# A weight conversion that begins one head pair later, with one of its steps in another cycle

## The chip, the cores and the metric

The kernel runs on one core of one Trainium2 chip. A core has five engines with a queue each: TensorE (PE), VectorE (DVE), ScalarE (ACT), GpSimd (POOL) and SyncE (SP, which here issues nearly all DMAs). The metric is the device time of one execution in microseconds; lower is better.

## The reference, cut to what matters

```python
# attention: batch 4, heads 8, sequence 576, head dimension 64
q_rot, k_rot = rotate(q), rotate(k)            # rotary embedding
scores = q_rot @ k_rot^T / 8
attn = softmax(scores)                         # row maximum subtracted first
x = (attn @ v) as (2304, 512)
# two FFN layers: weights 512 x 2048 and 2048 x 512, in float64
h = x @ w_in;   x = (h - tanh(h)) @ w_out
h = x @ w_in2;  out = (h * sigmoid(h)) @ w_out2
```

## The kernel before, in words

The 32 heads are taken as 16 **pairs** of heads. Each pair goes through five **cycles** (`z` from 0 to 4, here called cycle 1 to cycle 5). In a cycle TensorE multiplies the scores of two tiles (one in cycle 5; `sc`, L543), VectorE takes their row maxima (`row_max`, L548), ScalarE their exponentials (`exps`, L560). The score tiles have two buffers, so scores of one cycle wait for exponentials of the one before. In the same cycle TensorE transposes the probabilities of the cycles before (`tpp`, L453), which VectorE or ScalarE evict (L579, L581), multiplies them with v (L673), and `warm` (L519) issues transposes of the identity whose result nobody reads. GpSimd rotates q and k of a later pair (`rope_ops`, L416, L422, L426: three operations each). One rotation of pair 1 (numbered from 0) is done by VectorE instead. Its timeline in the first pair is one of the places that the change touches.

All engines take their work in the order in which this Python code issues it. Within a cycle the order is: scores and transposes, DMAs, early evictions, row maxima, VectorE's evictions, reciprocals, rotations, exponentials, late evictions, then `conv.run(n)`, then warm-up transposes and products with v.

`conv.run(n)` takes n steps of the **conversion** (class `Conv`, L92). The weights come as 64 float64 tiles of 128 by 512 (`keys`); of each, VectorE makes float32 bits in four operations: a single-operand one (`TENSOR_SCALAR`, L141) and three of two operands (L147, L152, L155). ScalarE squares the upper half (`magnitude`, L133). The first 16 tiles (`NEARLY`, j < 16) are then split into a high part by ScalarE (`high`, L166) and a low part by GpSimd (`low`, L170), and stay in SBUF. The later 48 go through DRAM (`wd`) and come back by `Fetch` (L200), which splits them (`split`, L254 and L255). The steps per cycle stand in `CONV_N`.

The FFN layers run in **ticks**: 160 of them, `tick(m)`. A tick multiplies one slice of h (`gemm_h`, L916, `hp`), issues its activations on ScalarE and VectorE, and then multiplies the slice of four ticks earlier with its second weight (`gemm_out`, L993, `acc`): for each of four column blocks three matmuls, high weight with high value, high weight with low value, low weight with high value. Before each use stands `need(key)`, which makes the fetcher go on until that weight has been issued. Otherwise the fetcher gets a number of turns per tick at the tick's end, and in the second part of the first layer only in some ticks:

```python
if TW[kb] == T and not (after and f % NH < 5):
    fetch.fill((2, int(f % NH > 3 or m < 5 * NH + NH), 3)[p])
```

For the ticks 40 to 47 that is one turn each, for 48 to 51 none, for 52 to 55 one each.

Of the kernel before, what the change touches and what calls it, by code (L numbers as in the profile page):

```python
# [29 lines left out]
def kernel(  # L30
# [34 lines left out]
    PE, ACT, DVE, POOL = nc.tensor, nc.scalar, nc.vector, nc.gpsimd  # L65
# [36 lines left out]
    class Conv:  # L102
# [33 lines left out]
        def bits(self, j):  # L136
            raw = self.raw[j]
            lo_w, hi_w = raw[:, :, 0], raw[:, :, 1]
            a = stage.tile([128, DM], I32, tag="wa", name="wa", bufs=3)
            af = self.val[j] = a.bitcast(F32)  # L140
            DVE.tensor_scalar(out=a, in0=hi_w, scalar1=3, scalar2=0x3FFFFFFF,  # L141
                              op0=ALU.logical_shift_left, op1=ALU.bitwise_and)
            yield
            if j < NEARLY:
                self.magnitude(j)
                yield
            DVE.scalar_tensor_tensor(out=a, in0=lo_w, scalar=29, in1=a,  # L147
                                     op0=ALU.logical_shift_right, op1=ALU.bitwise_or)
            if j >= NEARLY:
                self.magnitude(j)  # L150
            yield
            DVE.scalar_tensor_tensor(out=a, in0=hi_w, scalar=-0x40000000, in1=a,  # L152
                                     op0=ALU.bitwise_and, op1=ALU.bitwise_or)
            yield
            DVE.scalar_tensor_tensor(out=af, in0=self.mag.pop(j), scalar=TINY_HI * TINY_HI, in1=af,  # L155
                                     op0=ALU.is_ge, op1=ALU.mult)
            del self.raw[j]
            if j >= NEARLY:
                nc.sync.dma_start(out=wd[j], in_=self.val.pop(j))
                self.done = j + 1  # L160
            self.load(j + 3)
            yield
# [10 lines left out]
        def micro(self):  # L173

            late = []
            for j in range(self.n):
                if j >= NEARLY:
                    while late:
                        late.pop(0)()
                        yield  # L180
                while j >= self.allowed:
                    yield
                for n, _ in enumerate(self.bits(j)):
                    if late and n < 2:
                        late.pop(0)()
                    yield
                if j < NEARLY:
                    late += [lambda j=j: self.high(j), lambda j=j: self.low(j)]
# [137 lines left out]
    NP = B * NPAIR  # L326
# [3 lines left out]
    NPV = 4 * (NJ + 1)  # L330
    Q0 = 256
    WARM = (5, 5, 6, 2, 4, 1, 6)
    WARM_Z = (0, 6, 5, 5, 2, 0)
    ON_DVE = ((1, 0), (2, 0), (2, 1), (3, 0), (4, 0))
    QK_AT = (3, 2, 0)
    R_K = 3
    TURNED = mybir.DependencyInfo(mybir.DependencyClass.Sync, mybir.DependencyReason.DATA)
    E1_AT = 2
    PV_N = (4, 4, 6, 4, 2)
    CONV_N = (0, 0, 3, 2, 1), (2, 1, 1, 1, 1), (1, 1, 1, 1, 1)  # L340

    def attention(conv, on_rope_done, on_scores_near, on_scores_done):
        es_main, es_even, es_odd, es_rope, es_sc = (ExitStack() for _ in range(5))
# [38 lines left out]
        def load_v(i):  # L382
            b, c = divmod(i, NPAIR)
            vm = ap.tile([128, 2, NJ, D], F32, tag="vm", name="vm", bufs=2)

            vr = vr2[i % 2]
            nc.sync.dma_start(
                out=vm.rearrange("p h j d -> p h (j d)"),
                in_=v[b, 2 * c:2 * c + 2, 0:MAIN, :].rearrange("h (p j) d -> p h (j d)", j=NJ),
            )  # L390
            for h in range(2):
                nc.sync.dma_start(out=vr[half[h], h], in_=v[b, 2 * c + h, MAIN:S, :])
            v_t[i] = (vm, vr)
# [307 lines left out]
        pvq, rq, early, dve, late, stores = [], [], [], [], [], []  # L701

        def rope_push(i, ns=(4, 2, 3, 0, 1)):
            for n in ns:
                rq.extend((i, f) for f in rope_ops(i, n, POOL))
# [37 lines left out]
        conv.load(2)  # L743
        load_v(0)
        rope_push(1, (4, 3, 0, 1))
        i = z = 0
        while True:
            live, more = i < NP, i + 1 < NP
            qk_at = QK_AT[min(i, 2)]
            n0 = i * NTI + 2 * z  # L750
            gs = range(n0, n0 + (2 if z < NJ else 1)) if live else ()
            if more and z == 0:
                rope_upto(i + 1)
            early.clear(), dve.clear(), late.clear()
            pu = (i, z - 2) if z > 1 else (i - 1, z + NJ - 1)
            has = 0 <= pu[0] < NP
            if more and z == 0:
                qk_alloc(i + 1)
            qk = more and z == qk_at
            nop = nc.sync  # L760

            if len(gs) > 1:
                scores(gs[0], 0)
                if has:
                    turn(p_turn(*pu, 1))
                scores(gs[0], 1)
                blk = block(i, z)
                if blk:
                    t = turn(blk[1])
                scores(gs[1], 0)  # L770
                if qk and not blk:
                    kt = qk_turn(i + 1, 0)
                    tk = turn(kt[1])
                scores(gs[1], 1)
                if has:
                    turn(p_turn(*pu, 0))
                if blk:
                    turn_behind(t, blk[0], nop)
                if qk and blk:
                    kt = qk_turn(i + 1, 0)  # L780
                    tk = turn(kt[1])
                if qk:
                    turn_behind(tk, kt[0], nop)
            else:
                for g in gs:
                    scores(g, 0)
                    scores(g, 1)
                if live and more:
                    b = qk_turn(i + 1, 1)
                    up, dn = (p_turn(*pu, w) for w in (1, 0))  # L790
                    t = turn(b[1], dn[:NJ])
                    turn(up[:NJ], dn[NJ:])
                    n = nop.nop()
                    order(t, n)
                    order(n, turn(b[0][:1]))
                    turn(up[NJ:], b[0][1:])
                elif has:
                    turn(*[p_turn(*pu, w) for w in (1, 0)])
                blk = block(i, z)
                if blk:  # L800
                    turn_behind(turn(blk[1]), blk[0], nc.sync)
            store()
            if live:
                if i and z == 1:
                    load_v(i)
                if i == 0 and z == 1:
                    load_qk(2)
                if i + 3 < NP and z == 3:
                    load_qk(i + 3)
            if not n0:  # L810
                warm(WARM[5], idle)
                q_part(1, NJ)()
                warm(WARM[6], idle)

            for f in early:
                f()
            for g in gs:
                row_max(g)
            for f in dve:
                f()  # L820
            if i == 0 and z == 1:
                for f in rope_ops(1, 2, DVE):
                    f()
            if live and z == 2:
                recips(i, 0)
            if i and z == 0:
                recips(i - 1, 1)
            if more and z == (0 if i else 1) and i + 2 < NP:
                rope_push(i + 2)
            if live:  # L830
                for _ in range(4):
                    if rq:
                        rq.pop(0)[1]()
            if i == NP - 1 and z >= NJ - 1:
                on_scores_near(z)
            for g in gs:
                exps(g)
            for f in late:
                f()
            if live and z == NJ:  # L840
                pvq.extend((i, m) for m in range(NPV))
            conv.run(CONV_N[min(i, 2)][z] if i < NP else 0)
            if i * (NJ + 1) + z < len(WARM_Z):
                warm(WARM_Z[i * (NJ + 1) + z], idle)
            for _ in range(PV_N[z] if i < NP or z < 2 else NPV // 2):
                if pvq:
                    pv(*pvq.pop(0))
            if i >= NP - 1:
                store()
            if i == NP - 1 and z == 0:  # L850
                es_rope.close()
                es_even.close()
                on_rope_done()
            if i == NP - 1 and z == NJ:
                es_odd.close()
                es_sc.close()
                on_scores_done()
                on_tail()
            if not live:
                on_tail()  # L860
                if z > 1:
                    break
            i, z = (i, z + 1) if z < NJ else (i + 1, 0)
# [238 lines left out]
    conv = Conv()  # L1102
# [250 lines left out]
```

## Time and profile before

| | |
|---|---|
| median of 3 runs | 1067.76 us (1067.6 to 1068.08) |
| the profiled execution | 1068.44 us |
| its span, first to last instruction | 1066.7 us |
| PE busy | 1056.4 us, 99% of the span |
| DVE, ACT, POOL busy | 841.3, 631.7, 256.7 us |
| attention and its tail | to about 288 us |
| FFN layers | from then on, the first of their ticks in the tail |

Times in the rows below are microseconds from the span's start. A row of a timeline has the start, the duration, the engine, the line, the operation with the tiles that it writes and reads, their shape, and how many like instructions are merged in it; in brackets stands the idle time of the engine before it and what ended it. Line numbers are those of the kernel before; in the kernel after, lines 144 to 182 are one lower, and from 185 on two higher (746 to 820 three).

### The profile page before, as it was taken

To read this page: it belongs to the slowest core of one execution; us is meant where nothing else is said; L and a number is where in the kernel's file an instruction comes from. 1 tells how busy PE (TensorE), PEld (TensorE's weight loads), DVE (VectorE), ACT (ScalarE), POOL (GpSimd) and SP (SyncE) were. 2 spreads that over 40 slices of the span, in tenths; PEclk is the share of its full clock that TensorE was granted. 3 is DMA by queue.
4 is the path that set the end of the run, shared out by engine and by line. 5 is a ranking of instruction groups with operands and counts; after the bars stand their busy time and mean duration, and the time that the engine had idled before them with its cause. 6 is when DMAs were issued, how large, how long until landed. Compare 5 with 4: busy or idle time off the path is not lost.

```text
span 1066.7 us, 19432 instructions
## 1 busy us (share of the span) xinstructions
PE 1056.4 (99%) x7223; PEld 868.6 (81%) x7223; DVE 841.3 (79%) x1462; ACT 631.7 (59%) x1331; POOL 256.7 (24%) x324
## 2 busy tenths in 40 slices
PE   8999999999999999999999999999999999999998
PEld 6777777777688898888888898888888889999997
DVE  7889989988699778899999879977365357867775
ACT  5878777777667567768676666434343344334342
POOL 6888888882102001211020101400000000000000
PEclk9999999999999999999999999999999999999999
DMA  5334343333134323444555533756324212212142
GB/s 153 101 113 117 90 119 103 103 98 116 61 99 167 101 80 109 148 140 133 191 188 188 158 100 109 236 179 221 113 91 139 70 49 100 77 42 90 44 124 80
DMA packets 91278, 126.37 MB, mean 118 GB/s; under 512 B 16432, under 2 KB 57008, under 8 KB 91184
## 3 DMA queue, kind: packets, MB, share of 16 engines
q1 hardware_dynamic: 90592, 124.75, 36.7%
q8 instruction: 56, 0.92, 0.4%
q10 hardware_dynamic: 592, 0.39, 0.1%
q14 instruction: 38, 0.31, 0.1%
HBM read 88.93 MB, written 36.18 MB: 117 GB/s over the span
## 4 chain that ended last, share of the span: by engine, by line
PE 96%; ACT 2%; DVE 1%; issue 0%; SPq 0%; POOL 0%; DVEq 0%; POOLq 0%; ACTq 0%
PE hp L916 37%; PE acc L993 28%; PE M L1077 8%; PE sc L543 7%; PE x L673 6%; PE tpp L453 4%; PE tpq L453 2%; ACT p L560 1%; PE tpb L453 1%; PE acc L1221 1%; PE tpb L451 1%; DVE st L548 1%; PE x L519 0%; PE x L680 0%; PE x L677 0%
## 5 line engine op out<-in xcount | busy, mean ns | idle before, releaser
L916 PE MATMUL hp<-xh,w 128*128 128x512 f32 (+1 forms) x1280 | 388.0, 369 | 0.0
L916 PEld LDWEIGHTS hp<-xh,w 128*128 128x128 f32 x1280 | 234.5, 189 | 41.2 <-issue 0.8
L916 PE MATMUL hp<-xl,w 128*128 128x512 f32 (+1 forms) x640 | 236.0, 369 | 0.0
L927 ACT ACTIVATE t<-hp 128x512 f32<-128x512 f32 (+1 forms) x120 | 66.8, 557 | 243.3 <-PE hp L916 238.6
L993 PE MATMUL acc<-gh,w 128*128 128x512 f32 (+1 forms) x640 | 193.7, 368 | 0.0
L961 DVE TENSOR_TENSOR gl<-t,gh 128x512 fp32r<-128x512 f32 (+1 forms) x120 | 77.4, 645 | 111.8 <-ACT gh L959 111.5
L543 PE MATMUL sc<-kq 64*128 64x288 f32 (+1 forms) x640 | 151.4, 426 | 3.5 <-ACT p L560 2.6
L255 POOL TENSOR_TENSOR w<-wf,w 128x512 fp32r<-128x512 f32 x32 | 49.6, 1563 | 364.4 <-ACT w L254 364.4
L916 PEld LDWEIGHTS hp<-xl,w 128*128 128x128 f32 x640 | 120.8, 189 | 19.8 <-DVE xl L898 0.4
L993 PEld LDWEIGHTS acc<-gh,w 128*128 128x128 f32 x640 | 117.2, 189 | 20.3 <-issue 0.3
L548 DVE TENSOR_REDUCE st<-sc 128x1 f32<-128x576 f32 x144 | 107.5, 755 | 28.6 <-PE sc L543 23.4
L560 ACT ACTIVATE p<-sc,st 128x576 f32<-128x576 f32 x144 | 106.4, 740 | 37.7 <-DVE st L548 28.7
L993 PE MATMUL acc<-gl,w 128*128 128x512 f32 (+1 forms) x320 | 117.8, 368 | 0.0
L543 PEld LDWEIGHTS sc<-kq 64*128 64x128 f32 (+1 forms) x640 | 87.3, 176 | 36.1 <-ACT p L560 23.6
L453 PE MATMUL tpp<-ident,p 64*128 64x64 f32 x1248 | 101.7, 227 | 0.0
L453 PEld LDWEIGHTS tpp<-ident,p 64*128 64x128 f32 x1248 | 85.9, 139 | 4.1 <-DVE pt L581 2.5
L993 PE MATMUL acc<-w,gh 128*128 128x512 f32 x288 | 88.9, 390 | 0.0
L673 PE MATMUL x<-pt,vm 128*64 128x320 f32 (+1 forms) x512 | 79.5, 421 | 0.2 <-DVE xs L689 0.2
L959 ACT ACTIVATE gh<-t 128x512 fp32r<-128x512 f32 (+1 forms) x120 | 70.6, 588 | 6.2 <-PE acc L993 6.2
L1077 PE MATMUL M<-w,gh 128*128 128x256 f32 x384 | 70.3, 283 | 0.0
L993 PEld LDWEIGHTS acc<-gl,w 128*128 128x128 f32 x320 | 60.3, 189 | 9.9
L1077 PEld LDWEIGHTS M<-w,gh 128*128 128x128 f32 x384 | 61.8, 191 | 2.3
(140 smaller groups left out, 1950.7 us busy)
## 6 DMA issues: line engine op xcount, KB each, us to landing
raw<-in_moe_w_in_dram SPq DMA_DIRECT2D x32, 512.0 KB, 4.4
raw<-in_moe_w_out_dram SPq DMA_DIRECT2D x28, 512.0 KB, 3.7
xin<-xd SPq DMA_DIRECT2D x56, 256.0 KB, 4.1
wd<-wa SPq DMA_DIRECT2D x48, 256.0 KB, 2.2
wf<-wd SPq DMA_DIRECT2D x48, 256.0 KB, 4.0
pd<-xo SPq DMA_DIRECT2D x34, 256.0 KB, 2.7
xo<-pd SPq DMA_DIRECT2D x18, 256.0 KB, 5.2
xm<-in_q_dram SPq DMA_DIRECT2D x16, 256.0 KB, 3.0
```

The source lines that it names most:

```text
L255: (DVE if key[0] == 3 else POOL).tensor_tensor(out=w[:, 1].rearrange("p (a b) -> p a b", a=a), in0=src, in1=w[:, 0].bitcast(F32).rearrange ...
L453: t = PE.transpose(o, src, ident[r, r])
L543: PE.matmul(sc[o, e, 0:HALF], lhsT=kq[r, 1, c:c + n], rhs=kq[r, 0, k0:k0 + HALF], start=True, stop=True)
L548: DVE.tensor_reduce(out=st, in_=s_t[g][:, :, 0:HALF], op=ALU.max, axis=AX.XY, negate=True)
L560: ACT.activation(out=p.rearrange("p (e s) -> p e s", e=2), in_=sc[:, :, 0:HALF], func=ACTF.Exp, bias=st, accum_out=sum_t[i][:, n:n + 1])
L673: PE.matmul(x[o, 0:w], lhsT=vm[:, h, cc, :], rhs=ptm[:, cc, h, :], start=(cc == 0), stop=False)
L916: PE.matmul(hp, lhsT=w[:, a, ws], rhs=bb, start=(n == 0), stop=(n == 3 * KD - 1))
L927: ACT.activation(out=t, in_=hp, func=ACTF.Tanh, scale=0.5 if l else 1.0)
L959: ACT.activation(out=gh, in_=t, func=ACTF.Copy)
L961: DVE.tensor_tensor(out=gl, in0=t, in1=gh.bitcast(F32), op=ALU.subtract)
L993: PE.matmul(acc, lhsT=a, rhs=bb, start=(fi == 0 and n == 0), stop=(fi == NH - 1 and n == 2))
L1077: PE.matmul(prod_t[name][:, tt], lhsT=al[i], rhs=bw[j], start=(first and tt == 0 and x == 0), stop=(last and tt == nt - 1 and x == 2))
```

## The change

Four edits. In `bits`, ScalarE's squares of the first 16 tiles are issued in the same step as the single-operand operation, and not in a step of their own. In `micro`, the high part of the tile before gets a step of its own ahead of that. `CONV_N` becomes one step in cycle 5 of pair 0 and one step per cycle from then on; before, pair 0 had three, two and one steps in its cycles 3, 4 and 5, and pair 1 began with two. And VectorE's rotation of pair 1 is issued one operation per cycle in the cycles 1, 2 and 3 of pair 0, not as three in cycle 2, and the warm-up transposes of cycle 4 of pair 0 are 1 and not 5.

```diff
@@ bits @@
             DVE.tensor_scalar(out=a, in0=hi_w, scalar1=3, scalar2=0x3FFFFFFF,
                               op0=ALU.logical_shift_left, op1=ALU.bitwise_and)
-            yield
             if j < NEARLY:
                 self.magnitude(j)
-                yield
+            yield
@@ micro @@
-                for n, _ in enumerate(self.bits(j)):
-                    if late and n < 2:
+                if late:
+                    late.pop(0)()
+                    yield
+                for _ in self.bits(j):
+                    if late:
                         late.pop(0)()
                     yield
@@ tables @@
-    WARM_Z = (0, 6, 5, 5, 2, 0)
+    WARM_Z = (0, 6, 5, 1, 2, 0)
-    CONV_N = (0, 0, 3, 2, 1), (2, 1, 1, 1, 1), (1, 1, 1, 1, 1)
+    CONV_0 = (0, 0, 0, 0, 1)
@@ attention @@
         rope_push(1, (4, 3, 0, 1))
+        kr = rope_ops(1, 2, DVE)
         i = z = 0
...
-            if i == 0 and z == 1:
-                for f in rope_ops(1, 2, DVE):
-                    f()
+            if i == 0 and z < len(kr):
+                kr[z]()
...
-            conv.run(CONV_N[min(i, 2)][z] if i < NP else 0)
+            conv.run((1 if i else CONV_0[z]) if i < NP else 0)
```

On VectorE, pair 0, from the end of its preparation: `st` are the row maxima, `ak` and `bm` the rotation, `rr` the reciprocals, `wa` the conversion. Before:

```order
L508 TENSOR_TENSOR aq<-aq,p 128x2x3x64
L548 TENSOR_REDUCE st<-sc 128x1 x4
L416 TENSOR_TENSOR ak<-xm_192,csk 128x4x64
L422 TENSOR_TENSOR bm<-xm_192,csk 128x256
L426 TENSOR_TENSOR ak<-ak,bm 128x4x64
L548 TENSOR_REDUCE st<-sc 128x1 x2
L570 TENSOR_SCALAR rr<-sums 128x4
L571 RECIPROCAL rr<-rr 128x4
L141 TENSOR_SCALAR wa<-raw 128x512
L147 SCALAR_TENSOR_TENSOR wa<-raw,wa 128x512
L548 TENSOR_REDUCE st<-sc 128x1 x2
```

After:

```order
L510 TENSOR_TENSOR aq<-aq,p 128x2x3x64
L550 TENSOR_REDUCE st<-sc 128x1 x2
L418 TENSOR_TENSOR ak<-xm_192,csk 128x4x64
L550 TENSOR_REDUCE st<-sc 128x1 x2
L424 TENSOR_TENSOR bm<-xm_192,csk 128x256
L550 TENSOR_REDUCE st<-sc 128x1 x2
L428 TENSOR_TENSOR ak<-ak,bm 128x4x64
L572 TENSOR_SCALAR rr<-sums 128x4
L573 RECIPROCAL rr<-rr 128x4
L550 TENSOR_REDUCE st<-sc 128x1 x2
```

The three rotation operations stand each behind the maxima of one cycle, and no conversion step stands ahead of the maxima of cycle 4.

On VectorE from the maxima of cycle 4 of one pair to the first cycle of the next, as it then repeats from pair to pair. Before:

```order
L548 TENSOR_REDUCE st<-sc 128x1 x2
L581 COPY pr_690<-tpb 128x256
L581 COPY pt_689<-tpp 128x8x64
L141 TENSOR_SCALAR wa<-raw 128x512
L689 TENSOR_TENSOR xs<-x,rs 128x320
L548 TENSOR_REDUCE st<-sc 128x1
L581 COPY pt_836<-tpp 128x8x64 x2
L548 TENSOR_REDUCE st<-sc 128x1 x2
```

After:

```order
L550 TENSOR_REDUCE st<-sc 128x1 x2
L583 COPY pr_674<-tpb 128x256
L583 COPY pt_673<-tpp 128x8x64
L691 TENSOR_TENSOR xs<-x,rs 128x320
L550 TENSOR_REDUCE st<-sc 128x1
L583 COPY pt_818<-tpp 128x8x64 x2
L141 TENSOR_SCALAR wa<-raw 128x512
L550 TENSOR_REDUCE st<-sc 128x1 x2
```

The single-operand operation stood ahead of the one maximum of cycle 5 (and of the scaled output `xs`); it stands now behind the two evictions of that cycle and ahead of the maxima of the next pair's cycle 1.

On ScalarE in tick 51 of the FFN part: `t` is the tanh and `u` the square of the tick's `hp`, `xh` a split of the next input block, `w<-wf` the high part of a fetched weight. Names are shown with their numbers, which count up in the order of issue. Before:

```order
L897 ACTIVATE xh0_7699<-xin_7443 128x512
L927 ACTIVATE t_7703<-hp_7686 128x512
L931 ACTIVATE u_7705<-hp_7686 128x512
L959 ACTIVATE gh_7709<-t_7597 128x512
L940 ACTIVATE s_7713<-u_7705,sqa_70 128x512
L941 ACTIVATE mk_7714<-u_7705,ht2_71 128x512
L897 ACTIVATE xh1_7752<-xin_7444 128x512
L927 ACTIVATE t_7756<-hp_7739 128x512
```

After:

```order
L899 ACTIVATE xh0_7678<-xin_7421 128x512
L929 ACTIVATE t_7682<-hp_7665 128x512
L933 ACTIVATE u_7684<-hp_7665 128x512
L961 ACTIVATE gh_7688<-t_7575 128x512
L942 ACTIVATE s_7692<-u_7684,sqa_70 128x512
L943 ACTIVATE mk_7693<-u_7684,ht2_71 128x512
L256 ACTIVATE w_7698<-wf_7401 128x512
L899 ACTIVATE xh1_7745<-xin_7422 128x512
L929 ACTIVATE t_7749<-hp_7732 128x512
```

One row has come in, `w_7698`, behind the tick's own activations. On TensorE the matmuls that follow the tick's `hp` read that weight; before, they read one that was issued six ticks earlier (`w_7423`, in tick 45). Before:

```order
L916 MATMUL hp_7686<-xl3_7440,w_5709 128x512
L916 MATMUL hp_7686<-xh3_7439,w_5709 128x512
L993 MATMUL acc0_7352<-gh_7606,w_7423 128x512
L993 MATMUL acc0_7352<-gl_7607,w_7423 128x512
L993 MATMUL acc0_7352<-gh_7606,w_7423 128x512
```

After:

```order
L918 MATMUL hp_7665<-xl3_7418,w_5856 128x512
L918 MATMUL hp_7665<-xh3_7417,w_5856 128x512
L995 MATMUL acc0_7329<-gh_7583,w_7698 128x512
L995 MATMUL acc0_7329<-gl_7584,w_7698 128x512
L995 MATMUL acc0_7329<-gh_7583,w_7698 128x512
```

The matmuls stand where they stood; the weight that they read is issued just ahead of them. All other fetched weights are issued three ticks or more ahead of their use.

## Rows read from the trace of the kernel before

**Rows 1.** Timeline of PE in the first pair.

```profile
6.38 1.27 PE L519 MATMUL x<-ident 128*128 128x128 f32 x5
...
15.71 0.51 PE L543 MATMUL sc<-kq 64*128 64x288 f32 x1 [0.19 <-ACT p L560]
...
19.73 0.51 PE L543 MATMUL sc<-kq 64*128 64x288 f32 x1 [1.36 <-ACT p L560]
...
23.17 0.77 PE L519 MATMUL x<-ident 128*128 128x128 f32 x5
23.87 1.19 PE L543 MATMUL sc<-kq 64*64 64x288 f32 x8
```

**Rows 2.** Timeline of VectorE in the first pair.

```profile
14.03 1.48 DVE L548 TENSOR_REDUCE st<-sc 128x1 f32<-128x576 f32 x2 [1.72 <-PE sc L543]
15.43 0.97 DVE L416 TENSOR_TENSOR ak<-xm,csk 128x256 f32<-128x256 f32 x1
...
18.07 1.41 DVE L548 TENSOR_REDUCE st<-sc 128x1 f32<-128x576 f32 x2
```

**Rows 3.** Timeline of PE: first scores of cycles 1 and 2, pairs 2, 3, 14.

```profile
43.70 0.51 PE L543 MATMUL sc<-kq 64*128 64x288 f32 x1
...
47.12 0.51 PE L543 MATMUL sc<-kq 64*128 64x288 f32 x1
...
59.76 0.75 PE L543 MATMUL sc<-kq 64*128 64x288 f32 x2
...
63.38 0.51 PE L543 MATMUL sc<-kq 64*128 64x288 f32 x1
...
238.52 0.75 PE L543 MATMUL sc<-kq 64*128 64x288 f32 x2
...
242.16 0.51 PE L543 MATMUL sc<-kq 64*128 64x288 f32 x1
```

**Rows 4.** Timeline of VectorE around the starts of pairs 2 and 3.

```profile
43.26 1.29 DVE L581 COPY pt<-tpp 128x512 f32<-128x512 f32 x2
45.09 0.76 DVE L548 TENSOR_REDUCE st<-sc 128x1 f32<-128x576 f32 x1 [0.55 <-PE sc L543]
46.15 0.76 DVE L548 TENSOR_REDUCE st<-sc 128x1 f32<-128x576 f32 x1 [0.29 <-PE tpq L453]
...
57.58 0.97 DVE L141 TENSOR_SCALAR wa<-raw 128x512 int32<-128x512 int32 x1
...
59.53 1.27 DVE L581 COPY pt<-tpp 128x512 f32<-128x512 f32 x2
```

**Rows 5.** The line L141 over the span: ns shortest, median, longest.

```profile
L141 DVE TENSOR_SCALAR wa<-raw x64: 395/422/1522, 20.2 to 811.2; 128x512 int32<-128x512 int32 x64
```

**Rows 6.** Timeline of GpSimd around the start of pair 3.

```profile
57.53 0.73 POOL L426 TENSOR_TENSOR aq<-aq,bm 128x256 f32<-128x256 f32 x1
58.22 0.92 POOL L416 TENSOR_TENSOR aq<-xm,csq 128x256 f32<-128x256 f32 x1
...
60.59 1.28 POOL L170 TENSOR_TENSOR w<-wa,w 128x512 fp32r<-128x512 f32 x1
```

**Rows 7.** Timeline of ScalarE: first exponential of pair 2.

```profile
45.95 0.74 ACT L560 ACTIVATE p<-sc,st 128x576 f32<-128x576 f32 x1 [0.29 <-DVE st L548]
```

**Rows 8.** Timeline of ScalarE behind tick 51, and a weight's split in tick 52.

```profile
531.76 0.62 ACT L897 ACTIVATE xh<-xin 128x512 fp32r<-128x512 f32 x1
...
537.21 0.62 ACT L254 ACTIVATE w<-wf 128x512 fp32r<-128x512 f32 x1
```

**Rows 9.** Timeline of GpSimd, the low part of the same weight as in rows 8.

```profile
537.90 1.29 POOL L255 TENSOR_TENSOR w<-wf,w 128x512 fp32r<-128x512 f32 x1 [36.66 <-ACT w L254]
```

**Rows 10.** Timeline of PE in tick 51, from its first product with a second weight.

```profile
528.84 0.39 PE L993 MATMUL acc<-gh,w 128*128 128x512 f32 x1
...
529.29 0.62 PE L993 MATMUL acc<-gh,w 128*128 128x512 f32 x2
```

**Rows 11.** Stretches: busy us of PE, PEld, DVE, ACT, POOL; granted clock; DMA; GB/s.

```profile
1063.00:1066.70 3.70, 0.00 (x0) 0.00 (x0) 0.00 (x0) 0.00 (x0) 0.00 (x0) 0.88 0.46 126
```

## The prediction

> **What bounds the kernel now.** I read the page first: TensorE (PE) is busy for 99% of the span (the table above), so time is to be had only where PE stands still, and is lost wherever it is made to. The waits of PE and then its timeline show where that is. In the FFN layers its matmuls follow each other without a gap; in attention there are two places. The first is the first head pair: the scores of cycle 4 wait 1.36 us for an exponential [rows 1], and VectorE's timeline says why: the row maximum of cycle 3 starts at 18.07, behind three rotation operations that began at 15.43 [rows 2]. The second shows in no wait, only in a comparison of pairs: cycle 1 lasts 3.42 us in pair 2 (43.70 to 47.12), but 3.62 in pair 3 (59.76 to 63.38) and 3.64 in pair 14 (238.52 to 242.16) [rows 3]; all twelve pairs from 3 to 14 lie between 3.60 and 3.64. The reason is VectorE again: in pair 2's cycle 4 the single-operand step took 0.97 us where it mostly takes 0.42 [rows 4, 5], so that the two evictions of cycle 5 began 0.23 us ahead of the next pair's scores (59.53, 59.76) and not 0.44 (43.26, 43.70) [rows 3, 4]; PE's next transposes need the first eviction's bank. It took 0.97 because GpSimd was at work: GpSimd's operation ran from 57.53 to 58.26, and the step ended at 58.55, 0.29 after it [rows 4, 6].
>
> **The change part by part.**
> *Rotation, one step per cycle.* The first of the three operations goes into the 1.72 us that VectorE idles before 14.03 [rows 2]. The second stays ahead of cycle 3's maximum: 15.43 + 0.97 = 16.4, and the maximum can start when its scores are there, 1.39 us after the scores' start (43.70 to 45.09 [rows 3, 4]), so at 15.71 + 1.39 = 17.10, not 18.07. From such a start to the next scores it was 19.73 - 18.07 = 1.66 us [rows 1, 2], so cycle 4 starts at 18.76: 0.97 us won. The third operation lies behind that maximum, in time that the two conversion steps of cycles 3 and 4 leave empty.
> *Warm-up transposes 5 to 1 in cycle 4.* Five took 23.87 - 23.17 = 0.70 [rows 1]; four fewer are 0.56. They hid a wait before; with the maxima earlier there is none left to hide. Together 1.5; at least 0.6 if the maximum stays late, at most 1.9 with the small waits of cycle 4 gone too. I take **-1.6**.
> *The conversion begins one pair later.* Its operations are the same; only the first pair has fewer. In pairs 2 to 13 the one step that moves is the single-operand one: from ahead of cycle 5's maximum to behind cycle 5's evictions, ahead of the next pair's first maximum. Taking it away from its old place gives each of the twelve first cycles its 0.20 back (12 x 0.2 = 2.5 with the pairs as they are). What it meets at its new place decides. In pair 2's times: the evictions start at 59.76 - 0.44 = 59.32 and take 1.27, and an operation starts some 0.09 before the end of the one ahead, so the step comes at 60.50. GpSimd's operation at 58.22 is no longer held up and takes 0.73, not 0.92 [rows 6], so its subtraction for the weights starts at 60.59 - 0.19 = 60.40 and runs 1.28, to 61.68. It is ahead by 0.1; where the step came only 0.05 behind a GpSimd operation it waited it out [rows 4, 6], so it ends at 61.68 + 0.29 = 61.97. The row maximum behind it was wanted at 59.76 + 1.39 = 61.15 and starts at 61.88: 0.73 late. The chain to PE (0.86 to the exponential, its 0.74, some 0.14 more [rows 4, 7]) has 47.12 - 45.95 - 0.88 = 0.29 to spare, so PE is 0.44 late: the cycle takes 3.86, 0.24 more than now. The second maximum of that cycle waits for PE: it starts at 46.15, where 45.09 + 0.76 - 0.09 = 45.76 would do [rows 4], 0.39 to spare, so the reciprocals, from which GpSimd's round starts, slip by 0.73 - 0.39 = 0.34, 0.10 less than PE; in the next pair the subtraction ends 0.10 sooner, PE is 0.34 late, and there it stays: 3.76, or 0.14 more than now. 0.24 + 11 x 0.14 = **+1.8**. The bounds are -2.5 (the step gets through first) and +2.9 (0.24 each time).
> The Trainium skill, SBUF — State Buffer, section "Who interferes with whom", speaks against the new place: whichever of the two engines issues first holds the shared pair of ports for its whole instruction and the other fully blocks. The rows agree (an end 0.29 after GpSimd's); by it, too, the price hangs on the 0.1 alone. The sum by rule and by rows is one.
> *The backlog.* Attention now ends with weight 15 unfinished, and all 48 later weights are converted five steps later. Weight 15 itself is needed at tick 11 and emitted at tick 6. Most fetched weights are split one or two ticks later and still ticks ahead of use. One is not: the last second-half weight of the first FFN, ("out", 15). Its split was emitted in tick 45; now the fetcher has no turn left between ticks 48 and 51 (it gets none for the first four units of a block there), so it is emitted on demand in tick 51, directly before its first matmul: the order shows it behind tick 51's tanh and squares on ScalarE. Those wait for tick 51's own products, so the copy runs where ScalarE now does its next work, 531.76 [rows 8], to 532.38; GpSimd follows 0.69 after the copy's start and takes 1.29 (537.21, 537.90 [rows 8, 9]): 532.45 to 533.74. The third matmul of the group reads the low half; it started at 529.29, the first at 528.84 [rows 10]. With 0.1 for the signal (an estimate) the first can start at 532.48, 3.6 late, and the third at 533.84, 4.55 late. Forced conversion steps may hold GpSimd for a few tenths: up to 5.2. I take **+4.6**. Behind it on PE is everything else; nothing later gives it back, since PE has no idle time to shrink.
> *Sum.* -1.6 + 1.8 + 4.6 = +4.8. On the profiled execution's 1068.44 us (span 1066.7 and 1.7 around it) that is 1073.2; its time was 0.7 above the median, and on the median of 1067.76 it is **1072.5 us**.
>
> **Rivals.**
> *The step gets through before GpSimd (not slower).* My 0.1 us is made of several rows; if the subtraction starts 0.15 later than I have it, or the evictions end sooner, the step takes 0.42, ends at 60.9 before the maximum is wanted at 61.15, and each of twelve pairs wins 0.2 without loss: -1.6 - 2.5 + 4.6 = +0.5, so 1068.3. The timing repeats from pair to pair (3.60 to 3.64), so it is all of them or none. The 0.05 that decided in pair 2 speaks against it.
> *The clock falls in the pause of tick 51.* PE stands 3.6 us there. The trace has no fall between two matmuls, only one after the last: in 1063.0 to 1066.7 PE does nothing and the granted clock is 0.88 on the mean [rows 11]; with 1.0 and 0.5 as its two levels (2.4 and 1.2 GHz) it fell some 0.9 us before the end, 2.8 into that stretch. At the start five transposes still took 1.27 at 6.38, against 0.77 later [rows 1], so a low stretch could last 6.4 us and cost half of it: 1072.5 up to 1075.7.
> The Trainium skill, TensorE: Matmul & The Clock Gate, section "What's actually happening", has an idle array back at half its clock; no pause of this length lies between matmuls in this trace.
> *The weight is there in time.* If the split did not bind (ScalarE free earlier than its order allows), the sum is -1.6 + 1.8 = +0.2, 1068.0; with the step through as well, 1063.7. It needs the copy done by 528.84, before the products that stand ahead of it; the order leaves no way for that. That the first pair does not get shorter is no rival of its own: it adds 1.
>
> **How the numbers follow.** Forecast 0.54, with 1071.0 to 1073.8 as its own range (first pair 0.6 to 1.9, the pairs 1.2 to 2.9, the weight 4.4 to 5.2). Step through first: 0.24. Clock falls: 0.10. Weight in time: 0.08, half of it faster. Something else: 0.04. About 0.2%, 2.1 us, is what can be told from no change: slower means above 1069.9. Slower 0.54 + 0.10 + 0.02 = 0.66; same 0.24 + 0.04 + 0.01 = 0.29; faster 0.05. The range reaches from the step's rival to the lower part of the clock's: 1067.6 to 1074.4, which leaves out the faster cases and the longest low stretch.
>
> **What would show it.** Right: the waits of PE get two new rows of 3.6 and 0.9 us at L995, for the copy at L256 and the subtraction at L257; no wait of over 1 us stays in the first pair, whose second pair starts 1.6 us sooner; the step at L141 lasts 1.3 to 1.5 us in twelve pairs and overlaps the subtraction at L169; first cycles take 3.7 to 3.9. Wrong: steps of 0.4 us and first cycles of 3.42 (the first rival), no wait at L995, or a granted clock under 1.0 around 535.

## The result, and the profile of the kernel after

The kernel after takes 1074.74 us (median of 4 runs, 1074.6 to 1074.97) against 1067.92 of the kernel before (4 runs): the ratio is 1.0064, with a 95% interval of 1.0047 to 1.0082. It is slower, as forecast, but by 6.8 us and not by 4.7. The profiled execution of after took 1074.68 us with a span of 1072.9, 6.2 us longer than the span before; the rest of the difference is the 0.5 by which the profiled execution of before lay above its median.

The waits of PE in the kernel after show the two new rows at L995 and two more things.

```profile
PE sc L545 <- ACT p L562: 5.0, 16, 0.6
PE acc L995 <- ACT w L256: 3.4, 1, 3.4
PE x L521 <- POOL ident masks.py:199: 1.3, 1, 1.3
PE tpq L455 <- SPq L796: 0.9, 1, 0.9
PE acc L995 <- POOL w L257: 0.6, 1, 0.6
```

No wait of the first pair is over 1 us now (the 1.3 at L521 stands ahead of it, and stood there before). The first row had 5 waits of 2.6 us in all before; 11 of its 16 are new, each ahead of the scores of cycle 2, in the pairs 3 to 12 and 14. PE's timeline gives the places that answer to [rows 1, 3, 10]: first scores of pairs and cycles, the first product of the FFN layers, and tick 51.

```profile
8.86 1.25 PE L545 MATMUL sc<-kq 64*128 64x288 f32 x8
...
24.46 0.51 PE L545 MATMUL sc<-kq 64*128 64x288 f32 x1
...
57.00 0.51 PE L545 MATMUL sc<-kq 64*128 64x288 f32 x1
...
60.86 0.51 PE L545 MATMUL sc<-kq 64*128 64x288 f32 x1 [0.36 <-ACT p L562]
...
73.49 0.51 PE L545 MATMUL sc<-kq 64*128 64x288 f32 x1
...
77.26 0.51 PE L545 MATMUL sc<-kq 64*128 64x288 f32 x1 [0.29 <-ACT p L562]
...
221.28 0.27 PE L455 MATMUL tpq<-ident,aq 64*128 64x64 f32 x1 [0.95 <-SPq L796]
...
270.91 0.50 PE L918 MATMUL hp<-xh,w 128*128 128x512 f32 x1
...
528.61 0.39 PE L918 MATMUL hp<-xh,w 128*128 128x512 f32 x1
532.43 0.50 PE L995 MATMUL acc<-gh,w 128*128 128x512 f32 x1 [3.43 <-ACT w L256]
532.77 0.40 PE L995 MATMUL acc<-gl,w 128*128 128x512 f32 x1
533.78 0.93 PE L995 MATMUL acc<-gh,w 128*128 128x512 f32 x2 [0.62 <-POOL w L257]
534.51 0.63 PE L995 MATMUL acc<-gl,w 128*128 128x512 f32 x1
534.93 1.06 PE L995 MATMUL acc<-gh,w 128*128 128x512 f32 x2
535.79 0.63 PE L995 MATMUL acc<-gl,w 128*128 128x512 f32 x1
```

Pair 0 takes 24.46 - 8.86 = 15.60 us; before it took 17.65 (9.63 to 27.28). Pair 3's first cycle takes 3.86, where it took 3.62 [rows 3], and pair 4's 3.77. The FFN layers begin at 270.91; before they began at 270.94, so all of the attention part comes out even in these two executions. Two things that differ from one execution of a kernel to the next are in that: pair 0 begins 0.77 sooner (8.86 against 9.63; 9.45 in a second profile of the kernel after, below), and pair 12 loses 1.1 to a delayed DMA issue (last section). In tick 51 (which begins at 526.12, as before [rows 10]) the first product starts at 532.43 and the third at 533.78. From 534.51 on the starts lie 0.42 to 0.43 apart (534.51, 534.93; two of them to 535.79), where full speed is 0.23. The windows show why: granted clock in the column behind POOL.

```profile
526.12:531.56 5.44, 2.88 (x13) 2.06 (x11) 4.43 (x8) 3.91 (x8) 0.00 (x0) 1.00 0.90 291
531.56:534.00 2.44, 0.95 (x3) 0.51 (x4) 2.44 (x3) 1.33 (x3) 1.28 (x1) 1.00 0.08 31
534.00:537.50 3.50, 3.50 (x10) 2.72 (x10) 2.88 (x5) 0.00 (x0) 0.00 (x0) 0.52 0.40 106
537.50:543.00 5.50, 5.50 (x25) 4.54 (x24) 3.60 (x8) 2.28 (x5) 0.00 (x0) 0.99 1.00 357
```

PE's clock stood at 1.0 while PE waited and until 534, and then went to its lower level (0.5, 1.2 GHz) for some 3.4 us, in which PE was busy without a gap. Ticks 51 and 52 together take 17.12 us and not 10.88, 6.24 more: 4.49 from the late third product (533.78 against 529.29 [rows 10]) and 1.75 from the clock. That is as much as the spans differ by.

VectorE's timeline at the start of pair 3, which answers to [rows 4], and under it GpSimd's, which answers to [rows 6]:

```profile
56.56 1.29 DVE L583 COPY pt<-tpp 128x512 f32<-128x512 f32 x2 [0.22 <-PE tpp L455]
57.76 1.45 DVE L141 TENSOR_SCALAR wa<-raw 128x512 int32<-128x512 int32 x1
59.13 1.41 DVE L550 TENSOR_REDUCE st<-sc 128x1 f32<-128x576 f32 x2
```

```profile
56.97 0.72 POOL L428 TENSOR_TENSOR aq<-aq,bm 128x256 f32<-128x256 f32 x1
57.65 1.28 POOL L169 TENSOR_TENSOR w<-wa,w 128x512 fp32r<-128x512 f32 x1
```

The subtraction starts 0.11 ahead of the single-operand step and ends at 58.93; the step ends at 59.21, 0.28 after it, and the row maximum starts 2.13 after the pair's first scores (57.00).

### The profile page after: what moved, and what is told of

It reads as the page before. It is cut to its first block, busy times and chain, and to the rows that moved or that the text cites. A ratio compares the mean times of both kernels' runs of the same rounds, so it can differ in the third digit from the quotient of the medians.

```text
span 1072.9 us, 19417 instructions
## 1 busy us (share of the span) xinstructions
PE 1055.7 (98%) x7219; PEld 868.3 (81%) x7219; DVE 847.4 (79%) x1462; ACT 628.9 (59%) x1331; POOL 249.3 (23%) x324
## 4 chain that ended last, share of the span: by engine, by line
PE 89%; DVE 4%; issue 3%; ACT 2%; POOL 1%; DMA 0%; SPq 0%; ACTq 0%; POOLq 0%; DVEq 0%
PE hp L918 36%; PE acc L995 26%; PE M L1079 7%; PE sc L545 6%; PE x L675 5%; PE tpp L455 3%; ACT p L562 1%; DVE pt L583 1%; DVE wa L141 1%; PE tpq L455 1%; DVE st L550 1%; PE acc L1223 1%; PE tpb L455 1%; PE tpb L453 1%; DMA wf<-wd 0%
## 5 line engine op out<-in xcount | busy, mean ns | idle before, releaser
L995 PE MATMUL acc<-gh,w 128*128 128x512 f32 (+1 forms) x640 | 195.1, 370 | 4.0 <-ACT w L256 3.4
L995 PEld LDWEIGHTS acc<-gh,w 128*128 128x128 f32 x640 | 117.9, 190 | 25.4 <-ACT w L256 3.8
L257 POOL TENSOR_TENSOR w<-wf,w 128x512 fp32r<-128x512 f32 x32 | 45.8, 1440 | 355.6 <-ACT w L256 343.9
L995 PE MATMUL acc<-gl,w 128*128 128x512 f32 (+1 forms) x320 | 118.5, 370 | 0.0
L995 PE MATMUL acc<-w,gh 128*128 128x512 f32 x288 | 88.9, 390 | 0.0
L995 PEld LDWEIGHTS acc<-gl,w 128*128 128x128 f32 x320 | 60.7, 190 | 10.0
```

The lines of the kernel that those rows point to most:

```text
L257: (DVE if key[0] == 3 else POOL).tensor_tensor(out=w[:, 1].rearrange("p (a b) -> p a b", a=a), in0=src, in1=w[:, 0].bitcast(F32).rearrange ...
L995: PE.matmul(acc, lhsT=a, rhs=bb, start=(fi == 0 and n == 0), stop=(fi == NH - 1 and n == 2))
```

## The experiments

"Before" was run beside each group again, at 1067.97 to 1068.14 us. FFN ticks are compared from the start of tick 0 to the start of tick 158, 782.69 us in the kernel before and 788.96 in the kernel after.

**A turn in tick 48 that was none.** The condition was opened for tick 48, but the count beside it is zero there:

```diff
-            if TW[kb] == T and not (after and f % NH < 5):
+            if TW[kb] == T and (m == 6 * NH or not (after and f % NH < 5)):
```

> The kernel after with one turn of the fetcher in tick 48, so that the last second-half weight of the first FFN is split three ticks ahead of its use. Theory (the weight stall alone, and the low clock as its consequence): no wait of PE at L995 in tick 51, matmuls of 227 ns behind it, the tick 5.44 us long again, 6.2 us less than the kernel after: 1068.5 us. Rival 1 (the conversion as a whole is late): the stall turns up at another weight, 1072 or more. Rival 2 (the low clock has another cause than the pause): it stays, 1.7 us, at 1070.2.

1074.71 us (1074.13 to 1075.47): nothing moved. The edit gave no turn, so this is the kernel after once more and decides nothing on the stall. As a second profile of it it is of use: the same stall, but ticks 51 and 52 cost 6.90 us and not 6.24, since the low clock lasted longer (6.8 us). Pair 0 took 15.91, because its first cycle took 3.45 and not 3.14.

**The pause filled.** Matmuls whose result nobody reads stand ahead of the late weight's first product.

```diff
+        if m == 51:
+            fp = pools["h"].tile([128, T], F32, tag="h0", name="fp", bufs=1)
+            for _ in range(15):
+                PE.matmul(fp, lhsT=wtile[p, "in", f][:, 0, 0:128], rhs=xs_t[XAT[m], 0][0], start=True, stop=True)
```

> The kernel after with 15 matmuls whose result nobody reads ahead of the late weight's first product in tick 51, so that PE works through the 3.4 us in which it stood still. Theory (the clock fell because PE stood still): the first product starts at the same time as in the kernel after, but the granted clock stays 1.0 and the products behind it take 227 ns and not 427: 1.7 us less, 1073.0 us. Rival (the clock falls for another reason): the same low stretch, 1074.7.

1073.39 us (1073.23 to 1073.67). Windows of this run:

```profile
528.00:531.00 3.00, 3.00 (x14) 2.46 (x14) 1.99 (x5) 2.29 (x5) 0.00 (x0) 1.00 0.92 343
531.00:534.00 3.00, 1.80 (x7) 0.86 (x5) 2.96 (x5) 1.58 (x3) 1.82 (x1) 1.00 0.06 21
534.00:537.00 3.00, 2.99 (x13) 2.50 (x14) 2.96 (x5) 0.00 (x0) 0.00 (x0) 1.00 0.46 125
```

The clock stays at 1.0 although PE still waits 1.2 us for the low half; from 534 on 13 matmuls lie in 3 us, where the kernel after has 10 in 3.5. The gain is 1.35 us and not all of the clock's share, because here the low half's subtraction met a VectorE operation and took 1.82, 0.54 more. In all four executions the mean granted clock was 1.0. The low clock is a consequence of PE's pause.

**Half of it filled**, with 8 matmuls and not 15.

> The kernel after with 8 matmuls ahead of the late weight's first product and not 15: PE works through 1.8 us of the pause and stands still for 1.6. Theory (a pause of that length is not enough for the clock to fall): as with the pause filled, granted clock 1.0, 1073.0 to 1073.4. Rival (any pause of over a microsecond costs the clock): 427 ns products behind it, 1074.7.

1073.34 us, but in two groups: 1072.3 and 1072.51, 1074.17 and 1074.81. The profile is of the execution of 1074.17: PE waits 1.6 us, and the clock falls.

```profile
531.00:534.00 3.00, 1.47 (x5) 0.89 (x6) 2.97 (x4) 1.38 (x3) 1.28 (x1) 0.96 0.05 18
534.00:537.00 3.00, 3.00 (x9) 2.32 (x8) 2.38 (x4) 0.00 (x0) 0.00 (x0) 0.50 0.50 123
```

Neither theory holds as it was put. A wait of 1.6 us and one of 0.6 us behind it cost the clock in some executions and not in others (mean granted clock of the faster two 0.999 and 1.0, of the slower two 0.998).

**The step at its old place.** The single-operand step goes back to the end of cycle 4, with the old `bits` and `micro`, and one step more in pair 0.

```diff
-    CONV_0 = (0, 0, 0, 0, 1)
+    CONV_0 = (0, 0, 0, 1, 1)
```

> The kernel after with the single-operand step back at its old place (ahead of the maximum of cycle 5), with the conversion otherwise as late as in the kernel after; the stall of tick 51 stays. Theory (the step at its new place waits for GpSimd's subtraction and holds up the first maximum): the step takes 0.42 or 0.97 and not 1.4, first cycles of pairs 4 to 12 fall from 3.78 to 3.62, some 0.15 in each of eleven pairs and 0.24 in one: 1072.9 us, or 1071.8 if PE's wait for a delayed DMA issue in pair 12 does not come again. Rival (the place of the step is worth nothing): 1074.7, first cycles as in the kernel after.

1074.67 us, no gain. Yet the pairs behave as the theory says: first cycles of pairs 4 to 14 take 3.61 to 3.65, the pairs 16.24 to 16.28 and not 16.40, and pair 15 begins at 252.98, where the kernel with the pause filled, which has the same attention part as after, has 254.45. The gain is given back in pair 15. VectorE's timeline there:

```profile
266.79 1.28 DVE L898 TENSOR_TENSOR xl<-xin,xh 128x512 fp32r<-128x512 f32 x2
268.00 1.50 DVE L141 TENSOR_SCALAR wa<-raw 128x512 int32<-128x512 int32 x1
269.41 0.48 DVE L689 TENSOR_TENSOR xs<-x,rs 128x320 f32<-128x320 f32 x1
```

The step of weight 15, which before ran a pair earlier, meets GpSimd's subtraction (267.79 to 269.21), takes 1.50, and `xs` behind it comes late: a new wait of PE of 1.60 us at L673. Ticks 51 and 52 cost 7.54 in this execution, 3.05 of it for the clock.

**The rotation alone**, on the kernel before.

```diff
-            if i == 0 and z == 1:
-                for f in rope_ops(1, 2, DVE):
-                    f()
+            if i == 0 and z < len(kr):
+                kr[z]()
```

> The kernel before with VectorE's rotation of pair 1 issued one operation per cycle, and nothing else. Theory: the row maximum of cycle 3 comes 0.97 us sooner and the wait of 1.36 us ahead of cycle 4's scores falls to 0.4; the second pair starts 1.0 us sooner: 1066.9 us. Rival (the two conversion steps that stay ahead of cycle 4's maximum take the gain back, or the five warm-up transposes do): under 0.3 us, 1067.7.

1067.71 us, ratio 0.9997 (0.9988 to 1.0006): no change that can be told. Pair 0 takes 16.65 and not 17.65, the 1.00 of the theory; pair 1 takes 17.14 and not 16.42. There the two-operand step at L147 came at a time when GpSimd was busy, took 1.19 where it takes 0.65, and a new wait of 0.76 us stands ahead of cycle 3. The theory was right for pair 0; the rival had the size right, but the gain is not lost at the places that it named.

**The warm-up transposes**: the kernel after with five of them.

```diff
-    WARM_Z = (0, 6, 5, 1, 2, 0)
+    WARM_Z = (0, 6, 5, 5, 2, 0)
```

> The kernel after with the five warm-up transposes of cycle 4 of the first pair back (tick 51 as in the kernel after). Theory (four transposes are 0.56 us and nothing hides them any more): pair 0 takes 16.17 and not 15.61. Rival (they fill a wait): 15.6.

Pair 0 takes 15.98 and not 15.60: the four are worth 0.38 (the first cycle is 3.14 in both). (1075.12 us from two runs; the difference to 1074.74 is too small to be read from so few.)

**A turn in tick 48 that is one.**

```diff
-                fetch.fill((2, int(f % NH > 3 or m < 5 * NH + NH), 3)[p])
+                fetch.fill((2, int(f % NH > 3 or m < 5 * NH + NH + 1), 3)[p])
```

> The kernel after with one real turn of the fetcher in tick 48 (the edit before this one left the count for that tick at zero), which splits the late weight three ticks ahead of its use. Theory (the stall of tick 51 and the low clock behind it are the whole loss): no wait of PE at L995, granted clock 1.0 through tick 52, tick 51 5.44 us long, and the 6.2 to 6.9 us of the two executions profiled come back: 1068.0 us, even with the kernel before, since what the first pair wins the later pairs lose. Rival (a late conversion finds another weight): a wait of PE of over 1 us at another tick, 1070 or more.

1069.45 us (1067.95 to 1070.32). The waits at L995 in tick 51 are gone, tick 51 takes 5.44 and the clock stays at 1.0 from 526 on. But there is a new stall: tick 84 takes 6.02. VectorE's timeline there:

```profile
685.28 1.80 DVE L154 SCALAR_TENSOR_TENSOR wa<-wm,wa 128x512 f32<-128x512 f32 x1
687.00 2.47 DVE L1006 TENSOR_TENSOR xo<-acc,xo 128x512 f32<-128x512 f32 x4
```

A conversion step stands ahead of the four evictions of the `acc` banks that PE needs next, and takes 1.80 because GpSimd works on two low halves from 685.23 to 688.22. So the theory is right for tick 51 and the rival in kind: a late conversion finds another place, for 0.58 us in this execution. It was one of the fastest of eleven (1068.22 us); the median lies 1.3 above that of the run with the backlog cleared (below), and what the slower executions lost, and where, was not profiled.

**The step in a third place.** Together with that turn, the step of the next weight is issued behind the last step of the weight before, in cycle 3.

```diff
+        def first(self, j):
+            a = self.word[j] = stage.tile([128, DM], I32, tag="wa", name="wa", bufs=3)
+            DVE.tensor_scalar(out=a, in0=self.raw[j][:, :, 1], scalar1=3, scalar2=0x3FFFFFFF,
+                              op0=ALU.logical_shift_left, op1=ALU.bitwise_and)
...
             DVE.scalar_tensor_tensor(out=af, in0=self.mag.pop(j), scalar=TINY_HI * TINY_HI, in1=af,
                                      op0=ALU.is_ge, op1=ALU.mult)
+            if j < NEARLY - 1:
+                self.first(j + 1)
```

> The same turn in tick 48, and the single-operand step issued behind the last conversion step of the weight before, in cycle 3, ahead of the maxima of cycle 4, where VectorE idles 0.82 us. Theory (the step costs only by what it waits for and whom it holds up): nothing is ahead of the first maximum any more, first cycles of 3.42 in pairs 3 to 14 and not 3.78, pairs of 16.05: twelve times 0.36 below the run with the turn alone, 4.3 us: 1063.7 us. Rival (the step meets GpSimd's rotation there and holds up cycle 4's maxima in place of the first, past the 0.94 us that the scores have to spare): cycles 4 longer by what cycles 1 lose, 1067 to 1068.

1065.42 us, 4.0 below the run with the turn alone; ratio to before 0.9973 (0.9961 to 0.9984). All first cycles from pair 2 to 14 take 3.41 or 3.42, all pairs from 2 to 14 16.03 to 16.06. The step took 0.95 there (68.26 to 69.21 in pair 3), which cycle 4's maximum did not feel. Of the 1.7 us that are missing to 1063.7, 1.45 are those by which the run it starts from lay above its own 1068.0; tick 84 takes 6.89 here, as the same conversion step meets the same low halves.

**The backlog cleared.** Three conversion steps in the last pair's cycle 5 and one in each cycle of the tail, so that the FFN layers begin with weight 15 done, as before; no turn in tick 48.

```diff
-            conv.run((1 if i else CONV_0[z]) if i < NP else 0)
+            conv.run(1 + 2 * (i == NP - 1 and z == NJ) if i else CONV_0[z])
```

> The kernel after with the three steps that it leaves over from weight 15 run in the last pair's cycle 5 and the three that follow in the tail, so that the FFN layers begin with the conversion where it stood before; the fetcher is as in the kernel after, without the turn in tick 48. Theory (all of the loss in the FFN layers comes from the conversion that starts one weight behind): no stall in tick 51 or 84, ticks 0 to 157 take 782.7 us as before, and what is left is attention's sum of about zero: 1068.0 to 1068.8 us. Rival (the order of the FFN's work, not the backlog, makes the stall): 1074.

1068.13 us (11 runs), ratio 1.0001 (0.9993 to 1.001). No stall in the FFN layers, ticks 0 to 157 take 782.73. All of the change's loss in the FFN layers came from the conversion that starts one weight behind; without it the change is worth nothing.

**The subtraction out of the way.** As the run before, and GpSimd's subtraction issued one step later; the single-operand step stays at its new place.

```diff
-                for _ in self.bits(j):
-                    if late:
+                for n, _ in enumerate(self.bits(j)):
+                    if late and n:
```

> The run with the backlog cleared, and GpSimd's subtraction issued one step later, in the next pair's cycle 1 behind four rotation operations, with the single-operand step left at its new place. Theory (the step is dear because it waits for the subtraction): the step takes 0.42 behind cycle 5's evictions, first cycles of pairs 3 to 14 are 3.42 and not 3.78. Rival (any operation ahead of the first maximum costs the 0.36): first cycles stay at 3.78. The subtraction then lies in cycle 1 or 2 and may hold up VectorE there; the whole time is open, 1064 to 1070 us.

1063.95 us (1063.78 to 1064.2), ratio 0.9962 (0.9948 to 0.9976). VectorE's timeline at the start of pair 3:

```profile
57.11 1.29 DVE L583 COPY pt<-tpp 128x512 f32<-128x512 f32 x2 [0.22 <-PE tpp L455]
58.31 0.63 DVE L141 TENSOR_SCALAR wa<-raw 128x512 int32<-128x512 int32 x1
58.95 0.76 DVE L550 TENSOR_REDUCE st<-sc 128x1 f32<-128x576 f32 x1
```

The step takes 0.63, the maximum starts 1.40 after the pair's first scores (57.55), and first cycles take 3.41 or 3.42, every one from pair 2 to 14. It still ends 0.29 after an operation of GpSimd's, a rotation that ran from 57.92 to 58.65, but that is early enough. The place was never dear; the meeting with the subtraction was.

**Both repairs**, the step in cycle 3 and the backlog run off (one step more in each of the last pair's cycles 4 and 5, and one in each cycle of the tail).

> Both repairs: the single-operand step in cycle 3 behind the last step of the weight before, and the backlog run off in the last pair (one step more in its cycles 4 and 5) and the tail. Theory: attention as in the run with the early step (first FFN tick about 4 us sooner than in the kernel after), FFN layers as before without the 1.45 us at tick 84: 1063.9 us. Rival (the extra steps hold up the last pair or the tail): 1065 or more.

1063.91 us (1063.88 to 1064.21), ratio 0.9962 (0.9948 to 0.9975). Ticks 0 to 157 take 782.70. With the run before it this is the fastest version, 4 us below both kernels.

## Why the prediction was right and wrong

**First pair, -1.6: right, and a little short.** Pair 0 is 2.05 us shorter. The rotation gives the 0.97 that was worked out (1.00 alone), the transposes 0.38 and not 0.56. What is left, 0.67, was only in the upper bound: the conversion steps that no longer stand ahead of the maxima of cycles 4 and 5. Two runs together show that share: the rotation alone and the five transposes have the same rotation and the same transposes in pair 0 and differ in the conversion, and pair 0 takes 16.65 in the one and 15.98 in the other, 0.42 of it in cycle 4 and 0.26 in cycle 5. The step at its old place has the single-operand step ahead of cycle 5's maximum in pair 0 again, and pair 0 takes 15.61 there: that step alone costs nothing.

**The moved step, +1.8: right, by its mechanism and its numbers.** Forecast were a subtraction 0.1 ahead, a maximum 0.73 late, first cycles of 3.86 once and then 3.76; measured are 0.11, 2.13 - 1.39 = 0.74, 3.86 and 3.77 to 3.80. Over pairs 1 to 14 the kernel with the turn in tick 48 needs 229.40 us and the kernel before 227.52, +1.9. The rival by which the step gets through first came true nowhere, but its price did, where the subtraction was over before the step: at the start of pair 13 of the kernel after it ended at 222.97, the step came at 223.01, took 0.42, and the cycle 3.42; and the run with the subtraction moved has such cycles in every pair. By the Trainium skill, SBUF — State Buffer, section "Who interferes with whom", of GpSimd and a VectorE operation that uses both port pairs the one that issues first holds the shared pair for its whole instruction; the end 0.28 after GpSimd's (58.93, 59.21) agrees.

**The late weight, +4.6: right.** Forecast were the first product at 532.48 and the third at 533.84, 4.55 late; measured are 532.43 and 533.78, 4.49 late. The 0.1 for the signal had no row behind it; measured are 0.06 (the copy ends at 532.37) and 0.05 (the subtraction ends at 533.73). (The two rows of waits show 3.4 and 0.6 and not 3.6 and 0.9, since they count from the end of the matmul ahead, 528.61 + 0.39 = 529.00 for the first, while at full speed the next one starts before that end, at 528.84.)

**The clock: the step that failed.** It was a rival at 0.10, and its cost was left out of the sum. The reason given was that the trace has no fall between two matmuls; but from the first scores on PE's longest wait between two matmuls in the trace of before is 1.36 us, so that trace could not have one. The one row that bore on it gives the time from 1063.0 to the fall, 2.8 us [rows 11], but that is the edge of a stretch; PE had stopped sooner. Its last matmul before:

```profile
1061.76 0.39 PE L1221 MATMUL acc<-w,gl 128*128 128x512 f32 x1
```

It ended at 1062.15, so the clock fell 3.7 us after it, about as long as the pause of 3.6 that was forecast. A chance of 0.10 does not follow from that; it was not drawn from the row. (The ends of the other twelve profiles have the fall 2.1 to 5.2 us after the last matmul.) In all four profiles with the whole pause the clock fell, and it cost 1.75 us in the kernel after, 2.4 in its second profile, 3.05 with the step at its old place and 1.1 with five transposes; with the pause filled it did not fall. From medians: 1074.74 - 1068.13 = 6.6 for tick 51 in all, of which 4.5 is the pause, so 2.1 for the clock. The measured terms make -2.05 + 1.9 + 4.5 + 2.1 = 6.45 of the 6.8; the rest is no more than what executions of one kernel differ by here. Its own size was bounded rightly (up to 3.2), and the time lies inside that rival's 1072.5 to 1075.7; the range was cut at 1074.4 because its chance was too small. The Trainium skill, TensorE: Matmul & The Clock Gate, section "What's actually happening", which has an idle array back at half its clock, was right for this case (granted clock 0.52 from 534.0 to 537.5).

**The forecast's own range** of 1071.0 to 1073.8 is not what the bounds beside it add up to: -1.9 + 1.2 + 4.4 = 3.7 and -0.6 + 2.9 + 5.2 = 7.5, so 1071.4 to 1075.2. The measured time lies in that wider range, but it would be there by luck: the three terms came out at -2.05, 1.9 and 4.5, and what they leave open is the clock.

So attention won 2.0 us and lost 1.9, and nearly all of the 0.64% lies in two ticks of 160.

## What to carry to other kernels

A step that is postponed has to be followed to the last use of what it makes: here five steps of conversion cost nothing for 500 us and then hit the one weight that had no turn left. A free-looking slot is judged by which operation of the other engine that shares its ports is running at that moment: behind cycle 5's evictions the same step cost most pairs 0.36 beside the subtraction and nothing without it, and nothing behind cycle 3's last step. When a forecast contains a pause of PE of microseconds, the clock behind it belongs into the sum and not among the rivals: here 3.4 us cost it in four profiles of four, 1.6 us in two executions of four.

## What the runs showed of the hardware that was not expected

The fall of the clock can come well after the pause, when PE is at work again, or in the pause itself. In the kernel after PE stopped at 529.00, worked at 1.0 again from 532.43 and was slowed only from 534.1 to about 537.6. In its second profile (the turn in tick 48 that was none) PE stopped at 529.10 and started again at 532.52, and the clock fell ahead of that, at 531.9 (granted clock behind POOL):

```profile
530.00:531.00 1.00, 0.00 (x0) 0.00 (x0) 0.23 (x1) 1.00 (x3) 0.00 (x0) 1.00 1.01 387
531.00:532.00 1.00, 0.00 (x0) 0.00 (x0) 1.00 (x3) 1.00 (x3) 0.00 (x0) 0.94 0.42 160
532.00:533.00 1.00, 0.48 (x1) 0.48 (x2) 1.00 (x3) 0.99 (x2) 0.45 (x1) 0.50 0.01 2
```

In the four profiles with the whole pause the fall came 2.8 to 5.1 us after PE had stopped. The low stretch lasted 3.4 us in the kernel after and with five transposes (cost 1.75 and 1.1) and 6.8 us in the second profile and with the step at its old place (2.4 and 3.05). So what a pause costs differs by up to two microseconds between profiles with the same pause, and by 0.65 between the two of one kernel. With 1.6 us of pause the clock fell in the execution profiled, 1.9 us after PE had resumed; the times say that it fell in one more of the four.

SyncE held up PE in attention. In pair 12 of the kernel after, PE waits 0.95 us for SyncE (L796, an empty instruction that orders two groups of transposes through SyncE's queue). Its timeline:

```profile
217.28 0.42 SPq L368 DMA_DIRECT2D xm<-in_q_dram  x1
217.75 2.74 SPq L378 DMA_DIRECT2D xr<-in_q_dram  x1
220.54 0.62 SPq L378 DMA_DIRECT2D xr<-in_k_dram  x1
```

The issue of one 32 KB transfer took 2.74 us and not 0.63, and the empty instruction stood behind it. It cost pair 12 of this execution 1.1 us (17.53 against 16.41); the same issue took 1.94 in the second profile, where pair 12 took 16.71, and 2.38 with five transposes, where it took 17.15; where it took 1.50 or less the pair shows nothing of it. Why it takes longer was not tried and stays open.
